# Local attention's scores and values in one burst of matmuls, the linear state in another

## The chip, the core and the metric

The kernel runs on one core of a Trainium2 chip. The metric is the device time of one execution in microseconds (us); runs of one kernel are compared by their median. The engines are named as in the profile: PE (TensorE, matmuls) with PEld (its weight loads), ACT (ScalarE), DVE (VectorE), POOL (GpSimd) and SP (SyncE, which here issues most DMAs). Matmul results land in PSUM, eight banks of 128 partitions x 512 fp32 values.

## What is computed

One input x of 2048 positions x 1024 goes through two attention blocks of 32 heads of 32, and a gate mixes their outputs. Block A is linear attention, block B looks at eight positions, two apart, behind each query.

```python
g = sigmoid((x * gate_w).sum(-1, keepdims=True))
# A: phi(t) = where(t > 0, t + 1, exp(t)) + 1e-6
q, k, v = split(x @ A_wqkv); pq, pk = phi(q), phi(k)
kv = einsum("bhsd,bhse->bhde", pk, v); z = pk summed over s
a = (einsum("bhqd,bhde->bhqe", pq, kv) / (einsum("bhqd,bhd->bhq", pq, z) + 1e-6)) @ A_wo
# B: for query s the keys s, s-2, ..., s-14 (those >= 0)
q, k, v = split(x @ B_wqkv)
b = (softmax(q . k[idx] * 32**-0.5) over the 8 keys, times v[idx]) @ B_wo
out = g * a + (1 - g) * b
```

## The kernel before

A small planner (`Prog`) takes every operation in program order with an estimated cost, its reads and writes and a priority (by default the place in program order). It simulates the five engines and writes out a fixed order for each; waits between engines are semaphores that follow from reads and writes. It does so six times, each time giving out PSUM banks by when the pass before freed them, and keeps the shortest plan. PE, like the others, runs its list strictly in order.

The stages, in PE's order:

1. Values of B for all positions (L1413 to L1428), 16 tiles x 2 halves of 8 matmuls of 128x512 ("a group"), stored to HBM with a column of ones behind each head's 32 values (33 columns a head).
2. Keys and queries of B, transposed (L1540 to L1556), first for the even, then for the odd positions (`e_` = 0, 1; dilation 2 makes the two halves independent, and x is read so that each half lies together). 32 groups each. For `e_` = 0 the gate's products run on DVE beside them; for both, DVE keeps running maxima and minima of q and k (`top`).
3. Local attention of B, cut into 9 blocks of up to 2 x 57 queries for each half, 18 in all (`FILLS`). It is spread over the large groups: after each group `slot` is called, which adds `FILL` = 0.2 to a pace, so that every fifth group is followed by the `fill` of one block; `after(n, f)` calls f n slots later.
4. Keys of A through phi (L1590 to L1600, 32 groups, the key loop): ACT takes the exponential of the bank, DVE a minimum, and DVE adds both from the bank (`phi`, L1364).
5. The linear state. `mT` = x^T phi(k) (L1653 to L1666): 8 column chunks x 2 halves of 16 matmuls, against chunks `xn` of x loaded in natural layout. Then the state of each head, `W_v`^T `mT` (`state`, L1635), and its product with A_wo (`fold`, L1680).
6. Queries of A, their scaling by the denominators, and the outputs of both blocks (`query`, `scaled`, `output`).

One block of local attention (`fill`, L1469) goes so. `spread` (L1461) copies the block's queries into `qx` twice, once on ACT and once on DVE, each masked to every other head. 32 matmuls of 64x64 tiles (`s_fn`, L1480) write the scores of 64 keys x 114 queries into the four banks `SO` = 4 to 7. ACT takes the exponential of the four banks into `E` (L1489), DVE multiplies the band mask on (L1492), and then `spread` is put into the program for the next block. Three slots later `values` (L1498) follows: 64 matmuls of 33 columns into the same four banks, the last column of a head being the softmax denominator; DVE takes the reciprocal of the denominators (L1514), multiplies (L1515), and two DMAs store the block to HBM, from where `turn` (L1454) reads finished tiles back transposed into `qT`, the left operand of the outputs. Large groups meanwhile take banks from `main` = banks 0 to 3 (L1445).

The state is made in eight pieces: three slots after each chunk of `mT`, `state(c)` adds the chunk's 32 matmuls of 128x32 tiles to one bank that DVE set to zero before; that bank is kept back from `main` (banks 0 to 2) while the `mT` loop runs. After the first two query groups of A the bank is copied to `kvT` (L1754), which `fold` reads.

At the start of the key loop (L1565 to L1587) DVE reduces the maxima and minima (`top_end`), which go to HBM and back as one row to make a flag: the kernel branches on it late, into a general path that the data don't take. The two first `xn` chunks (four DMAs) are loaded there too; their memory overlaps that of the maxima and of the gate's tiles.

Of the kernel before, what the change touches and what calls it, by code (L numbers as in the profile page):

```python
# [6 lines left out]
ACT = mybir.ActivationFunctionType  # L7
# [8 lines left out]
DH = 32  # L16
# [1103 lines left out]
def build_kernel(nc, A_x, A_wqkv, A_wo, B_x, B_wqkv, B_wo, gate_w, out):  # L1120
# [110 lines left out]
    rs = SB([128, 4, 8], F32, "rs")  # L1231
    ao = Ring([SB([128, 4, 8, 32], BF16, "ao%d" % i) for i in range(2)])
# [31 lines left out]
    def plan(seen):  # L1264
# [5 lines left out]

        class Pool:


            def __init__(self, bs):
                self.bs, self.n = bs, 0

            def next(self):
                if seen is None:
                    b = self.bs[self.n % len(self.bs)]
                else:  # L1280
                    b = min((b for b in self.bs if b.take is None or b.take in P.read), key=lambda b: seen[b.take] if b.take is not None else -1.0)
                self.n += 1
                b.take = len(takes)
                takes.append(len(P.ops))
                return b
# [36 lines left out]
        def top_end(i, op):  # L1322
            P.op("dve", lambda e: e.tensor_reduce(mx4[:, i:i + 1], mx[i][:, :], AX.X, op), 0.15 + mx[i].row / 960.0, reads=[mx[i].all()], writes=[mx4.part((i, i + 1))])
# [121 lines left out]
        main = Pool(banks[0:4])  # L1445
# [15 lines left out]
        def spread(e_, qs, nq, offs):  # L1461
            ready.append((e_, qs))
            rd = [pick.all(), qT.part((0, 8), (e_ * HS + qs, e_ * HS + qs + 2 * nq))]
            to = lambda i: qx[:, i, :, 0:2 * nq]
            of = lambda: qT[:, :, e_ * HS + qs:e_ * HS + qs + 2 * nq]
            P.op("act", lambda e: e.activation(to(0), of(), ACT.Copy, scale=pick[:, 0:1]), act(16 * nq), reads=rd, writes=[qx.part((0, 1), (0, 8), (0, 114))])
            P.op("dve", lambda e: e.tensor_scalar(to(1), of(), pick[:, 1:2], None, op0=ALU.mult), 0.1 + 16 * nq / 1920.0, reads=rd, writes=[qx.part((1, 2), (0, 8), (0, 114))])

        def fill(e_, qs, nq, offs):  # L1469
# [10 lines left out]
            def s_fn(e):  # L1480
                for c in range(8):
# [5 lines left out]
            P.op("pe", s_fn, 0.6, mode="r", reads=[kT.part((0, 8), (t0 + k0[0], t0 + k0[1] + 64)), qx.all()], writes=[s.iv for s in SO], name="S")  # L1487
            E, _ = Er.next()
            P.op("act", lambda e: e.activation(E[:, 0:32 * nq].rearrange("p (j q) -> p j q", j=4), ps[:, 4:8, 0:8 * nq], ACT.Exp), act(32 * nq),  # L1489
                 reads=[s.iv for s in SO], writes=[E.all()])  # L1490
            ev = lambda: E[:, 0:32 * nq].rearrange("p (g q) -> p g q", g=16)
# [3 lines left out]
            if todo:  # L1495
                spread(*todo[0])

            def values():  # L1498

                def each(e):  # L1500
                    for i in range(16):
                        for h in range(2):
                            for g in range(2):
                                hd = 16 * g + i
                                c, j = hd // 4, hd % 4
                                at = (j // 2 * 16 + 2 * c + j % 2) * nq
                                last = e.matmul(SO[2 * h + i // 8].ap(i % 8 * 33, i % 8 * 33 + 33)[64 * g:64 * g + nq, :], E[64 * h:64 * h + 64, at:at + nq],  # L1507
                                                vt[64 * h:64 * h + 64, hd * 33:hd * 33 + 33], start=True, stop=True, tile_position=(64 * h, 64 * g))
                    return last
                bi = [s.iv for s in SO]  # L1510
                P.op("pe", each, 0.6, mode="c", reads=[vt.all(), E.all()], writes=bi, name="PV")
                o_, k = ao.next()
                pv = lambda lo, hi: ps[:, 4:8, 0:264].rearrange("p b (i d) -> p b i d", d=33)[:, :, :, lo:hi]
# [345 lines left out]
```

## Time and profile before

| | us |
|---|---|
| median of 3 runs | 483.25 (482.88 to 484.38) |
| profiled execution | 483.49 |
| its span | 481.8 |

Busy time by stage of the profiled execution, as the profile counts it:

| stretch (us) | what runs | PE | DVE | ACT | POOL |
|---|---|---|---|---|---|
| 125.4 to 181.1 | odd keys and queries, local attention | 55.70 | 44.57 | 22.37 | 0.00 |
| 181.1 to 243.5 | key loop, local attention | 62.40 | 50.58 | 33.31 | 0.00 |
| 243.5 to 309.2 | `mT`, state, local attention | 65.70 | 28.40 | 22.48 | 32.94 |
| 339.1 to 442.7 | outputs and queries of A | 103.60 | 79.97 | 14.71 | 0.00 |

How to read the lines that follow: a group of instructions is named by line, engine and operation, then written tile <- read tiles, shapes and a count ("x32"), then total busy time in us and the mean of one in ns, then the engine's idle time before them and what ended it. The chain of waits is the work that ended last, followed back from the end; its pieces show start, length, engine and line. Matmuls are pipelined: the length shown for one is from its start to its modelled end, and matmuls in a row overlap, so distances between starts say what one costs. All matmuls of `group` have line L1360, whatever stage calls it.

### The profile page before, as it was taken

How to read it: one execution, taken by the hardware profiler on the slowest of the kernel's cores; microseconds unless marked ns; L12 is line 12 of the kernel's file. 1: busy time of each engine (PE TensorE's matmuls, PEld its weight loads, DVE VectorE, ACT ScalarE, POOL GpSimd, SP SyncE). 2: the span in 40 equal slices, each digit the busy share in tenths (PEclk: the TensorE clock that was granted, in tenths of full speed). 3: DMA queues.
4: the chain of work that ended last, by engine and by line, in shares of the span. 5: the costliest groups of instructions: out<-in, count | busy, mean ns of one | idle time of the engine just before them, and what ended most of it. 6: DMA issues, size and time to landing. Idle time of an engine off the chain costs nothing.

```text
span 481.8 us, 9606 instructions
## 1 busy us (share of the span) xinstructions
PE 476.6 (99%) x4162; PEld 224.9 (47%) x4162; DVE 308.9 (64%) x513; ACT 129.8 (27%) x176; POOL 39.4 (8%) x40
## 2 busy tenths in 40 slices
PE   9999999999999999999999999999999999999996
PEld 6444444444444444444444444444444444444444
DVE  2212176799877789877773325399987777677512
ACT  2111111112333435556533343244221000110000
POOL 3000000000000000000068551100000000000000
PEclk9999999999999999999999999999999999999999
DMA  9999998233123354373138554661423111241111
GB/s 237 214 215 289 327 321 245 73 102 98 35 57 74 103 136 110 87 184 74 46 87 197 138 141 88 172 191 33 89 66 66 44 45 44 71 63 44 46 44 48
DMA packets 95116, 57.09 MB, mean 118 GB/s; under 512 B 55385, under 2 KB 88538, under 8 KB 95066
## 3 DMA queue, kind: packets, MB, share of 16 engines
q1 hardware_dynamic: 94234, 55.61, 44.3%
q10 hardware_dynamic: 832, 0.79, 0.6%
q8 instruction: 34, 0.56, 0.5%
q14 instruction: 16, 0.13, 0.1%
HBM read 30.56 MB, written 12.72 MB: 90 GB/s over the span
## 4 chain that ended last, share of the span: by engine, by line
PE 99%; DVE 0%; issue 0%
PE ps_all L1360 58%; PE ps_all L1733 23%; PE ps_all L1661 12%; PE ps_all L1507 2%; PE ps_all L1484 2%; PE ps_all L1396 1%; PE ps_all L1640 1%; PE ps_all L1688 0%; DVE o L1390 0%
## 5 line engine op out<-in xcount | busy, mean ns | idle before, releaser
L1360 PE MATMUL ps_all<-w,xT 128*128 128x512 bf16 x512 | 113.1, 379 | 0.0
L1360 PE MATMUL ps_all<-xT,w 128*128 128x512 bf16 x512 | 112.6, 379 | 0.0
L1360 PEld LDWEIGHTS ps_all<-xT,w 128*128 128x128 bf16 x512 | 49.1, 98 | 58.5
L1360 PEld LDWEIGHTS ps_all<-w,xT 128*128 128x128 bf16 x512 | 48.9, 98 | 57.8
L1366 ACT ACTIVATE e<-ps_all 128x512 bf16<-128x512 f32 x64 | 38.2, 597 | 118.5 <-PE ps_all L1360 115.5
L1733 PE MATMUL ps_all<-kT,aT 128*128 128x512 bf16 (+1 forms) x264 | 60.7, 373 | 0.0
L1733 PE MATMUL ps_all<-w,qT 128*128 128x512 bf16 (+1 forms) x264 | 60.7, 373 | 0.0
L1360 PE MATMUL ps_all<-kT,xT 128*128 128x512 bf16 x256 | 57.9, 379 | 0.0
L1661 PE MATMUL ps_all<-pk,xn 128*128 128x512 bf16 x256 | 57.8, 380 | 0.0
L1387 DVE CAST vst<-ps_all 128x512 bf16<-128x512 f32 x16 | 11.1, 694 | 44.6 <-PE ps_all L1360 44.6
L1733 PEld LDWEIGHTS ps_all<-w,qT 128*128 128x128 bf16 x264 | 25.8, 98 | 29.7
L1733 PEld LDWEIGHTS ps_all<-kT,aT 128*128 128x128 bf16 x264 | 25.7, 98 | 29.5 <-issue 0.2
L1360 PEld LDWEIGHTS ps_all<-kT,xT 128*128 128x128 bf16 x256 | 24.7, 98 | 30.0 <-issue 0.7
L1390 DVE TENSOR_SCALAR o<-ps_all,gm 128x512 bf16<-128x512 f32 (+1 forms) x27 | 19.7, 731 | 28.2 <-PE ps_all L1733 28.2
L1661 PEld LDWEIGHTS ps_all<-pk,xn 128*128 128x128 bf16 x256 | 23.9, 98 | 27.6
L1489 ACT ACTIVATE E<-ps_all 128x1824 bf16<-128x1824 f32 (+1 forms) x18 | 30.4, 1688 | 16.7 <-PE ps_all L1484 16.7
L1367 DVE TENSOR_SCALAR e<-e 128x512 bf16<-128x512 bf16 x64 | 18.7, 294 | 23.2 <-ACT e L1366 23.1
L1623 POOL TENSOR_TENSOR zacc<-zacc,pk 128x1024 f32<-128x1024 f32 x15 | 31.9, 2127 | 16.3 <-DVE E L1492 15.5
L1388 ACT ACTIVATE kT<-ps_all 128x512 bf16<-128x512 f32 x24 | 13.8, 597 | 42.4 <-PE ps_all L1360 39.2
L1492 DVE TENSOR_TENSOR E<-E,msk 128x1824 bf16<-128x1824 bf16 (+1 forms) x18 | 20.5, 1140 | 4.1 <-ACT E L1489 4.1
L1388 ACT ACTIVATE vst<-ps_all 128x512 bf16<-128x512 f32 x16 | 9.6, 600 | 48.8 <-PE ps_all L1360 48.8
L1369 DVE SCALAR_TENSOR_TENSOR pk<-ps_all,e 128x512 bf16<-128x512 f32 x32 | 21.8, 685 | 0.7
(65 smaller groups left out, 343.3 us busy)
## 6 DMA issues: line engine op xcount, KB each, us to landing
v<-vB_hbm SPq DMA_DIRECT2D x36, 132.0 KB, 5.0
vB_hbm<-vst SPq DMA_DIRECT2D x32, 132.0 KB, 5.0
w<-in_B_wqkv_dram SPq DMA_DIRECT2D x4, 1024.0 KB, 9.4
xt<-in_A_x_dram SPq DMA_DIRECT2D x16, 256.0 KB, 5.4
w<-in_A_wqkv_dram SPq DMA_DIRECT2D x4, 1024.0 KB, 10.1
xn<-in_A_x_dram SPq DMA_DIRECT2D x8, 512.0 KB, 5.4
out_dram<-o SPq DMA_DIRECT2D x15, 256.0 KB, 2.0
oB_hbm<-ao SPq DMA_DIRECT2D x32, 114.0 KB
```

Source lines behind the costliest of these rows:

```text
L1360: last = e.matmul(bank.ap(), lhs(dc), rhs(dc), start=(dc == 0), stop=(dc == 7))
L1366: P.op("act", lambda e: e.activation(e_[:, :], bank.ap(), ACT.Exp), act(512), reads=[bank.iv], writes=[e_.all()])
L1367: P.op("dve", lambda e: e.tensor_scalar(e_[:, :], e_[:, :], 1.0, 1e-6, op0=ALU.min, op1=ALU.add), 0.25, reads=[e_.all()], writes=[e_.all()])
L1369: P.op("dve", lambda e: e.scalar_tensor_tensor(out=dst, in0=bank.ap(), scalar=0.0, in1=e_[:, :], op0=ALU.max, op1=ALU.add), dps(512), read ...
L1387: fd = lambda e: e.tensor_copy(dst, src())
L1388: fa = lambda e: e.activation(dst, src(), ACT.Copy)
L1390: fd = lambda e: e.tensor_scalar(dst, src(), scale, None, op0=ALU.mult)
L1489: P.op("act", lambda e: e.activation(E[:, 0:32 * nq].rearrange("p (j q) -> p j q", j=4), ps[:, 4:8, 0:8 * nq], ACT.Exp), act(32 * nq), rea ...
L1492: mk = P.op("dve", lambda e: e.tensor_tensor(ev(), ev(), m[:, :, :].rearrange("p r q -> p (r q)")[:, None, :].to_broadcast([128, 16, 2 * n ...
L1623: P.op("pool", lambda e, t=t: e.tensor_tensor(zacc[:, :], zacc[:, :], pkS[:, t, :], ALU.add), 2.2, reads=[src, zacc.all()], writes=[zacc.a ...
L1661: last = e.matmul(bank.ap(), tl[:, t, cs:cs + 128], pkS[:, t, r * 512:(r + 1) * 512], start=(t == 0), stop=(t == NT - 1))
L1733: last = e.matmul(bank.ap(0, f1 - f0), lh[:, k, t * 128:(t + 1) * 128], w[:, k, f0:f1], start=(first and k == 0), stop=(not first and k == 7))
```

## The change

- The values of a block no longer have a burst of their own. `fill` puts them into `pending`, and the next block's `burst` issues its 32 score matmuls and then the 64 value matmuls of the block in front as one PE operation. The first block's scores and the last block's values (three slots after its scores) stay alone.
- The values get banks of their own: 14 of 16 heads of each group go to `VO` = banks 2 and 3, the last two to columns 456 to 488 of the four `SO` banks, behind the scores. So a burst needs six banks. `Pool` gets `soon`: while a burst is two slots away or less, large groups may take banks 0 and 1 alone.
- The results are four DVE instructions (reciprocal and product for the 14, then for the 2); `rs` and `ao` are laid out anew for it. They come in the program behind the exponential of the scores of the same burst and ahead of its mask.
- `spread` for the next block comes three slots after the scores, and both its copies wait for the last PE operation planned by then.
- `top_end` halves its 1024 columns twice by `tensor_tensor` and reduces 256; the two calls, the flag's chain and the first `xn` loads come 6, 11, 12 and 12 slots into the key loop.
- The state's 256 matmuls are one PE operation after the first two query groups of A, and its order is changed: for each four heads all eight chunks in a row, the first of them starting the sum. The zeroed bank is gone, `main` has four banks in the `mT` loop (under the rule of `soon`), and the copy to `kvT` follows the burst.

```diff
-    rs = SB([128, 4, 8], F32, "rs")
-    ao = Ring([SB([128, 4, 8, 32], BF16, "ao%d" % i) for i in range(2)])
+    rs = SB([128, 2, 16], F32, "rs")
+    ao = Ring([SB([128, 2, 16, 32], BF16, "ao%d" % i) for i in range(2)])
...
             def next(self):
+                bs = self.bs[0:2] if self.soon is not None and self.soon() <= 2 else self.bs
...
         def top_end(i, op):
-            P.op("dve", lambda e: e.tensor_reduce(mx4[:, i:i + 1], mx[i][:, :], AX.X, op), 0.15 + mx[i].row / 960.0, reads=[mx[i].all()], writes=[mx4.part((i, i + 1))])
+            behind = [[o for o in P.ops if o.eng == "pe"][-1]]
+            for n in (512, 256):
+                P.op("dve", lambda e, n=n: e.tensor_tensor(mx[i][:, 0:n], mx[i][:, 0:n], mx[i][:, n:2 * n], op), 0.08 + n / 1920.0, reads=[mx[i].all()], writes=[mx[i].all()],
+                     after=behind)
+            P.op("dve", lambda e: e.tensor_reduce(mx4[:, i:i + 1], mx[i][:, 0:256], AX.X, op), dps(256), reads=[mx[i].all()], writes=[mx4.part((i, i + 1))])
...
         SO = banks[4:8]
-        main = Pool(banks[0:4])
+        VO = banks[2:4]
+
+        def soon():
+            if todo:
+                return max(1, int(-(-(1.0 - pace[0] - 1e-6) // FILL)))
+            return later[0][0] - slot_n[0] if pending and later else 99
+
+        main = Pool(banks[0:4], soon)
+        pending = []
+        pace = [0.0]
+        P.op("dve", lambda e: e.memset(SO[3].ap(456, 489), 1.0), 0.1, writes=[SO[3].iv])
...
+        def burst(s_fn, reads, cost):
+            v_fn, v_reads, results = pending.pop() if pending else (None, [], None)
+            for b in (VO if v_fn else []) + SO:
+                take(b)
+
+            def fn(e):
+                last = s_fn(e) if s_fn else None
+                return v_fn(e) if v_fn else last
+            P.op("pe", fn, cost + (0.48 if v_fn else 0.0), mode="r", reads=reads + v_reads, writes=[b.iv for b in (VO if v_fn else []) + SO], name="S" if s_fn else "PV")
+            if results:
+                afterwards.append(results)
...
-            P.op("pe", s_fn, 0.6, mode="r", reads=[kT.part((0, 8), (t0 + k0[0], t0 + k0[1] + 64)), qx.all()], writes=[s.iv for s in SO], name="S")
+            burst(s_fn, [kT.part((0, 8), (t0 + k0[0], t0 + k0[1] + 64)), qx.all()], 0.4)
...
+            while afterwards:
+                afterwards.pop()()
...
             if todo:
-                spread(*todo[0])
...
+                after(3, lambda f=todo[0]: spread(*f, behind=[[o for o in P.ops if o.eng == "pe"][-1]]))
+
+            def v_fn(e):
+                for i in range(16):
+                    for h in range(2):
+                        for g in range(2):
+                            hd = 16 * g + i
+                            c, j = hd // 4, hd % 4
+                            at = (j // 2 * 16 + 2 * c + j % 2) * nq
+                            to = VO[h].ap(i * 33, i * 33 + 33) if i < 14 else SO[2 * h + i - 14].ap(456, 489)
+                            last = e.matmul(to[64 * g:64 * g + nq, :], E[64 * h:64 * h + 64, at:at + nq],
+                                            vt[64 * h:64 * h + 64, hd * 33:hd * 33 + 33], start=True, stop=True, tile_position=(64 * h, 64 * g))
+                return last
...
+                for i0, i1, src, bs in ((0, 14, pv, vb), (14, 16, px, xb)):
+                    reg = [rs.part((h, h + 1), (i0, i1)) for h in range(2)]
+                    P.op("dve", lambda e, i0=i0, i1=i1, src=src: e.reciprocal(rs[:, :, i0:i1], src(32, 33).rearrange("p a b o -> p a (b o)")), 0.2, reads=bs, writes=reg)
+                    P.op("dve", lambda e, i0=i0, i1=i1, src=src: e.tensor_tensor(o_[:, :, i0:i1, :], src(0, 32), rs[:, :, i0:i1, None].to_broadcast([128, 2, i1 - i0, 32]), ALU.mult),
+                         dps(64 * (i1 - i0)), reads=bs + reg, writes=[o_.part((h, h + 1), (i0, i1), (0, 32)) for h in range(2)])
...
-            after(PVLAG, values)
...
+            def finish():
+                burst(None, [], 0.0)
+                afterwards.pop()()
+
+            pending.append((v_fn, [vt.all(), E.all()], results))
+            if not todo:
+                after(PVLAG, finish)
...
-        top_end(0, ALU.max)
-        top_end(1, ALU.min)
...
+        after(6, lambda: top_end(0, ALU.max))
+        after(11, lambda: top_end(1, ALU.min))
...
+            for o in P.ops[first:]:
+                o.prio += 40 if o.eng == "dve" else 0
+
+        after(12, fast_ok)
...
-        xns = [load_xn(0), load_xn(1)]
+        xns = []
+        after(12, lambda: xns.extend(load_xn(i) for i in range(2)))
...
-        main = Pool(banks[0:3])
-        sb = banks[3]
-        sb.take = len(takes)
-        takes.append(len(P.ops))
-        P.op("dve", lambda e: e.memset(sb.ap(0, 256), 0.0), dps(256), writes=[sb.iv])
-
-        def state(c):
+        def state():
+            sb = main.next()
+
             def fn(e):
                 for i in range(8):
-                    for j in range(4):
-                        h = 4 * i + j
-                        last = e.matmul(sb.ap()[32 * j:32 * j + 32, i * 32:i * 32 + 32], ws[0][:, c, h * 32:(h + 1) * 32], mT[:, c, h * 32:(h + 1) * 32],
-                                        start=False, stop=(c == 7), tile_position=(0, 32 * j), skip_group_check=True)
+                    for c in range(8):
+                        for j in range(4):
+                            h = 4 * i + j
+                            last = e.matmul(sb.ap()[32 * j:32 * j + 32, i * 32:i * 32 + 32], ws[0][:, c, h * 32:(h + 1) * 32], mT[:, c, h * 32:(h + 1) * 32],
+                                            start=(c == 0), stop=(c == 7), tile_position=(0, 32 * j))
                 return last
-            P.op("pe", fn, 0.22, mode="c", reads=[ws[0].part((c, c + 1), (0, 1024)), mT.part((c, c + 1), (0, 1024))], writes=[sb.iv], name="kv")
+            P.op("pe", fn, 2.1, mode="c", reads=[ws[0].all(), mT.all()], writes=[sb.iv], name="kv")
+            move(kvT[:, :, :].rearrange("p i d -> p (i d)"), lambda: sb.ap(0, 256), 256, sb, kvT.all())
...
-            after(3, lambda c=c: state(c))
...
-        move(kvT[:, :, :].rearrange("p i d -> p (i d)"), lambda: sb.ap(0, 256), 256, sb, kvT.all())
+        state()
```

72 lines of the change are left out of this document (33 added, 39 removed).

## The prediction

> **What bounds the kernel now.** I read the page's busy shares, clock and chain first, then the pieces of the chain in order of time, then single bursts.
>
> ```profile
> PE 476.6 (99%) x4162; PEld 224.9 (47%) x4162; DVE 308.9 (64%) x513; ACT 129.8 (27%) x176; POOL 39.4 (8%) x40
> PEclk9999999999999999999999999999999999999999
> q8 instruction: 34, 0.56, 0.5%
> PE 99%; DVE 0%; issue 0%
> ```
>
> TensorE is 99% of the chain, at full clock in every slice. No other engine's time is on the path, so the change is worth what it does to TensorE's own sequence, plus any wait that it brings in. The sequence itself, from the chain of waits (start, us, line, matmuls):
>
> ```profile
> 125.44 0.53 PE ps_all L1484 x32
> 125.97 5.29 PE ps_all L1360 x24
> 131.25 0.61 PE ps_all L1507 x64
> 131.87 3.56 PE ps_all L1360 x16
> ...
> 161.22 0.74 PE ps_all L1507 x64
> ...
> 243.67 1.73 PE ps_all L1661 x8
> ...
> 257.75 0.30 PE ps_all L1640 x32
> 261.61 0.61 PE ps_all L1507 x64
> 262.22 0.31 PE ps_all L1640 x32
> ...
> 312.83 0.31 PE ps_all L1640 x32
> ...
> 339.30 6.91 PE ps_all L1733 x32
> 346.20 3.45 PE ps_all L1360 x16
> ```
>
> The rows join end to end: between the scores (L1484), the values (L1507), the state (L1640) and the large matmuls nothing waits. One thing is paid beside arithmetic. Sixteen large matmuls take 3.45 where nothing lies between them and 3.56 where a burst follows; 24 take 5.29 against 6.91 x 24/32 = 5.18. So entering a burst costs 0.11. What leaving one costs lies inside the burst's own piece:
>
> ```profile
> 125.37 0.60 PE L1484 MATMUL ps_all<-qx,kT 64*64 64x114 bf16 x32
> 131.19 0.68 PE L1507 MATMUL ps_all<-v,E 64*57 64x33 bf16 x64
> 257.68 0.38 PE L1640 MATMUL ps_all<-mT,w 128*32 128x32 bf16 x32
> L1484 PE MATMUL ps_all<-qx,kT x576: 207/209/237, 125.4 to 299.1; 64*64 64x114 bf16 x172, 64*64 64x112 bf16 x20
> L1507 PE MATMUL ps_all<-v,E x1152: 174/178/200, 131.2 to 305.3; 64*57 64x33 bf16 x172, 64*56 64x33 bf16 x20
> L1640 PE MATMUL ps_all<-mT,w x256: 176/176/190, 257.7 to 313.0; 128*32 128x32 bf16 x128
> 131.18:131.51 0.33, 0.33 (x43) 1.00 0.00 0
> ```
>
> The first three are from the timeline, the next three give the length of one matmul (min/median/max, ns), the last counts the L1507 matmuls active in a stretch. A burst's length less one matmul is the time from its first start to its last: scores 0.60 - 0.21 = 0.39, values 0.68 - 0.18 = 0.50, state 0.38 - 0.18 = 0.20. The piece of the scores is 0.53, so 0.14 lie between its last start and the next large matmul. The last round of four needs 114 columns, at 6.91/32 = 0.216 per 512 columns 0.05; leaving costs 0.09. For the values it is 0.61 - 0.50 = 0.11, less a round of 0.03: 0.08.
>
> **The joined burst.** 576/32 = 18 score bursts and 1152/64 = 18 value bursts stand now. A pair costs 0.53 + 0.61 + 2 x 0.11 = 1.36. Afterwards the first scores and the last values stay alone and 17 bursts hold 32 + 64 matmuls. Both kinds work in 64-by-64 tiles (the 57 and 56 columns of the values fit a 64-wide one). If no turn is paid between them, a joined burst is 0.11 + 0.39 + 0.05 + 0.50 + 0.03 + 0.08 = 1.16: 0.20 saved, 3.4 for the 17. No row shows scores followed directly by values. The other end is that the turn stays. A state burst behind values pays none of the 0.11 in its neighbours' pieces (0.61, then 0.31), yet 0.61 is what values cost before large matmuls too: one turn of 0.08 to 0.09 between two kinds of tile instead of two. By that end a pair saves 0.11, the 17 save 1.9. I take 3.4, since the rows show turns only where the tile's shape changes (64x64, 128x32, 128x128) and none inside the values, whose four positions alternate. [...]
>
> **The state.** Eight bursts of 0.30 to 0.31 (the first and the last stand above) are 2.44; five follow another burst directly, three stand alone (257.75 and 312.83 are two of them) and pay 0.11 each: 2.77 together. One burst pays entry and exit once, 0.19. Its 256 matmuls cost 0.20/31 = 0.0065 each if they go on as 32 do: 1.6, a gain of 1.0. Against that, of the values 43 fall into the first 0.33, and the other 21 start in the 0.18 up to 131.69: 0.0086 each. A long burst slows down once it has run some 43 deep, and by that price 256 take 2.20. Then there is the piece of 0.74 among those of 0.61, 0.13 more with no engine named: I read it as a hitch in the supply of instructions, since a matmul and its weight load are two instructions of 64 bytes if the instruction queue's 0.56 MB in 34 packets carry them all (8,324), and one packet of 16 KB is 128 matmuls. Two such hitches in 256: 0.26. Together 2.65, a gain of 0.1, which I take, as 256 lie far past 43. [...] That consecutive matmuls of the new order add to the same 32 columns is in no row of small tiles; it is a rival below. Its copy to SBUF stays two large groups (3.45) ahead of the first fold that reads it.
>
> **What is costed at nothing, and its cover.** TensorE's queue holds all the large matmuls behind a burst, so any late input of a burst is paid in full.
>
> ```profile
> 215.40:225.40 10.00, 10.00 (x141) 4.79 (x144) 7.65 (x14) 5.46 (x7) 0.00 (x0) 1.00 0.36 65
> 211.20 0.68 PE L1507 MATMUL ps_all<-v,E 64*56 64x33 bf16 x64
> 211.30 0.60 ACT L1366 ACTIVATE e<-ps_all 128x512 bf16<-128x512 f32 x1 [1.13 <-PE ps_all L1360]
> 212.37 1.21 DVE L1515 TENSOR_TENSOR ao<-ps_all,rs 128x1024 bf16<-128x1024 f32 x1
> 213.50 0.68 DVE L1369 SCALAR_TENSOR_TENSOR pk<-ps_all,e 128x512 bf16<-128x512 f32 x1
> L1489 ACT ACTIVATE E<-ps_all 128x1824 bf16<-128x1824 f32 x16 | 27.1, 1691 | 15.1 <-PE ps_all L1484 15.1
> L1492 DVE TENSOR_TENSOR E<-E,msk 128x1824 bf16<-128x1824 bf16 x16 | 18.3, 1146 | 3.6 <-ACT E L1489 3.6
> L1466 ACT ACTIVATE qx<-qT,pick 128x912 bf16<-128x912 bf16 x16 | 16.7, 1047 | 2.0 <-DVE qT L1390 2.0
> L1514 DVE RECIPROCAL rs<-ps_all 128x32 f32<-128x32 f32 x18 | 6.4, 356 | 17.2 <-PE ps_all L1507 17.2
> ```
>
> Banks: the last two of the five groups ahead of a burst may take only banks 0 and 1, and the burst needs 2 and 3 read. Now the key group that ends at 211.1 has its bank read at 213.50 + 0.68, 3.1 later, behind a value result of 1.21. Afterwards the last group before a burst has the burst and one group, 1.16 + 1.73 = 2.9, until its bank is wanted, and value results begin only 1.2 after its end, when its chain (0.60, 0.3, 0.68 and the steps between, 1.9) is nearly through. The group just behind the burst is worse: the exponential (1.69) holds ScalarE, then results and mask (1.15) hold VectorE; by these rows its bank is read some 3.2 to 3.4 after its end, and group four wants it at 2 x 1.73 = 3.45. Covered, with little to spare.
>
> Copies of the queries (1.05 on ScalarE) move from right behind the scores to after the third group, which leaves two groups, 3.45, for 1.05 plus one 0.60 ahead of it. The results become four VectorE instructions for two, 0.3 to 0.4 more per burst by the 0.36 of a reciprocal of 32 columns, against 10.00 - 7.65 = 2.35 idle in such a stretch. The two long reductions of the maxima are cut into halvings and a short reduction and go 6 and 11 groups later; they fill the same idle time. ScalarE's exponential and mask start 0.55 later in the burst but have five groups until the values read them, where they had three.
>
> SyncE: four xn loads, the write and the read-back of the three maxima move 12 groups (some 23 us) into the key loop, whose 32 groups end at 243.67 and begin some 62 earlier. The read-back waits for the write on SyncE's queue, with v loads and result stores behind it:
>
> ```profile
> 184.29 0.57 SPq L1569 DMA_DIRECT2D mx_hbm<-mx  x1
> 188.48 0.23 SPq L1570 DMA_DIRECT2D mxr<-mx_hbm  x1
> DMA to landing us min/median/max: 3.7/5.4/8.0
> ```
>
> That is a hold of 4.2 before, and the same after, against the 9.8 from one burst to the next. The xn loads (8.0 at most to land) would start near 205 and are read by L1661 at 243.67. If that cover were gone, each microsecond late would be one on the path.
>
> **The sum.** The profiled execution took 483.49, its span 481.8, the rest lies outside. 483.49 - 3.4 - 0.1 = 480.0. The median of the three runs, 483.25, is 0.24 below it, so I forecast 479.8. Less than 0.3%, 1.45, could not be told from no change.
>
> **The rivals.**
> *The turn between scores and values stays.* 1.9 in place of 3.4: 481.5, as a median 481.3. For it: every row where one burst meets another shows a turn. Against: in all of them the tile's shape changes.
> *The state burst outruns its instructions.* Two 16 KB blocks are used in 2.2, while a fetch packet takes 0.5% x 16 x 481.8/34 = 1.13. With both fully exposed the state costs 0.19 + 2.20 + 2.26 = 4.65, 1.9 over now: 482.0, as a median 481.8.
> *Banks.* If the bank read of 3.4 slips past 3.45 by 0.5 in the six bursts of the key loop, where each bank needs two engines, 3.0 come back: 483.0, as a median 482.8. For it: the margin of 0.1. Against: VectorE idles a quarter of that stretch, and the other 11 bursts have single copies to read a bank.
> *Slower: the state's sums wait for themselves.* In L1640's new order eight rounds in a row add to the same columns. If each round must see the last one written, it costs one matmul's length, 0.176, in place of 0.026 to 0.034: 64 x 0.176 + 0.19 = 11.5 against 2.77, and 483.49 - 3.4 + 8.7 = 488.8, as a median 488.6. It decides from a round of 0.093 up ((3.4 + 2.77 - 0.19)/64), where the gain is gone. Against: large matmuls add to the same bank at 0.216 apart with no wait; for it, 0.026 is a spacing at which the trace has no such sum.
> That scores and values don't come together is excluded: they are one operation of the plan.
>
> **How the numbers follow.** Forecast 0.56, turn 0.15, instructions 0.08, banks 0.09, sums 0.08, anything else 0.04. The forecast's own range is 478.9 (state at its fast price) to 480.6 (a pair saves 0.15). The range asked for reaches over the turn, the instructions and the banks to 482.8 and down to 478.7. Faster by over 0.3% (under 481.8): 0.55 + 0.12 + 0.05 + 0.03 + 0.02 = 0.77. Slower: 0.08 + 0.02 of the banks + 0.02 = 0.12. The rest, 0.11, is no change.
>
> **What would show it.** In the chain: 17 pieces of 96 matmuls at about 1.05 (1.16 less the entry), near 1.15 with the turn; the piece ahead still 5.29 or 3.56; one L1640 piece of 256 at about 2.5, near 4.5 with fetches, over 10 with waiting sums. A bank wait would show as ScalarE or VectorE in the chain, or as a TensorE piece of 8 to 24 large matmuls longer than its count x 0.216 + 0.11. I am wrong if the joined pieces don't save 0.2 each, or if such longer pieces add up to over 2.

## The result, and the profile after

| | before | after |
|---|---|---|
| median of the runs side by side (us) | 483.25 (9 runs) | 487.35 (486.02 to 491.11, 9 runs) |
| ratio, 95% interval | | 1.0099 [1.0072, 1.0126] |
| profiled execution, its span | 483.49, 481.8 | 488.77, 486.9 |

The kernel became 1.0% slower; the forecast was 479.8. The profiled execution of the changed kernel lies 1.4 above its median, so the sizes below are those of a longer execution than most; its runs spread over 5 us, those of before over 1.8.

From the page of the changed kernel, busy times and the chain that ended last:

```profile
PE 470.9 (97%) x4115; PEld 227.3 (47%) x4162; DVE 316.5 (65%) x555; ACT 129.9 (27%) x174; POOL 40.2 (8%) x40
PE 95%; DMA 2%; issue 2%; DVE 1%
```

TensorE was 99% of the chain and is 95% now, with a DMA and VectorE in it. So the loss is waits, not matmuls. Where the joined bursts run undisturbed, the chain (start, us, line, matmuls) reads:

```profile
145.24 0.53 PE ps_all L1518 x32
145.77 0.51 PE ps_all L1542 x63
146.28 0.16 issue
146.44 8.58 PE ps_all L1368 x39
155.02 0.53 PE ps_all L1518 x32
```

Of each burst's 64 value matmuls and of the 40 large ones one record is missing, which the chain shows as 0.16 of issue. A cycle of five groups is 155.02 - 145.24 = 9.78; before it was 0.53 + 5.29 + 0.61 + 3.56 = 9.99. That is 0.21 a pair, 3.6 for 17. That scores pass into values without a turn is read from the starts in the timeline below: 213.59 and 214.03 are 0.44 apart, the 0.39 + 0.05 of the prediction, and nothing is left for the 0.09 of a turn.

The first loss lies in the key loop. The chain there:

```profile
203.90 0.52 PE ps_all L1518 x32
204.42 0.51 PE ps_all L1542 x63
...
205.08 5.14 PE ps_all L1368 x23
...
210.35 6.80 DMA mx_hbm<-mx
...
217.17 4.71 DMA mxr<-mx_hbm
...
221.90 0.65 DVE mx L1619
...
224.03 5.30 PE ps_all L1368 x16
229.33 0.53 PE ps_all L1518 x32
```

And the timeline of the same stretch (start, length, instruction; in brackets the idle time before it and who ended it):

```profile
213.59 0.60 PE L1518 MATMUL ps_all<-qx,kT 64*64 64x114 bf16 x32
...
214.03 0.67 PE L1542 MATMUL ps_all<-v,E 64*56 64x33 bf16 x64
...
217.04 1.69 ACT L1523 ACTIVATE E<-ps_all 128x1824 bf16<-128x1824 f32 x1 [2.74 <-PE ps_all L1368]
...
217.97 3.63 PE L1368 MATMUL ps_all<-w,xT 128*128 128x512 bf16 x16 [1.44 <-DVE pk L1377]
...
221.90 0.65 DVE L1619 TENSOR_REDUCE mx<-mxr 1x3 f32<-1x384 f32 x1 [1.91 <-DMA mxr<-mx_hbm]
...
224.01 2.38 PE L1368 MATMUL ps_all<-w,xT 128*128 128x512 bf16 x7 [2.41 <-DVE mx L1624]
```

The flag's maxima go to HBM in 6.80 and come back in 4.71, 11.5 together where the trace of before has 4.2 for the write. VectorE reaches the reduction of the row (L1619) at 219.99 (221.90 - 1.91) and stands until the row is there. The reads of the banks are behind it in VectorE's fixed order, TensorE has no bank to write, and stands 2.41. Some 5 us ahead there is another stand of 1.44: the joined burst's last matmul starts near 214.5, yet ScalarE's exponential and VectorE's reciprocal, which wait for its signal, start together at 217.04. In the trace's signals TensorE's own comes 2.5 behind the last start; behind every other burst it is 0.24. Behind both comes a third cost (window, TensorE busy; the 0.50 is the granted clock):

```profile
224.85:228.26 3.41, 3.41 (x9) 1.22 (x8) 1.74 (x5) 0.60 (x1) 0.00 (x0) 0.50 0.80 184
```

For 3.41 TensorE has half its clock and does 1.7 of work. From 203.90 to 229.33 two cycles take 25.43 in place of 19.56: 5.9 lost, as 1.6 + 2.6 + 1.7 (the stands as distances of starts less one matmul, 0.2 over the idle times).

The second loss is the state (chain; then the instruction queue in the stretch 315.4 to 318.5, packets, MB, share of 16 engines):

```profile
310.06 3.45 PE ps_all L1368 x16
313.52 1.88 PE ps_all L1690 x200
315.40 3.07 issue
318.47 0.59 PE ps_all L1690 x56
319.06 0.16 issue
319.22 3.40 PE ps_all L1368 x15
```

```profile
q8 instruction: 1, 0.02, 2.2%
```

200 matmuls go in 1.88, then nothing for 3.07 with no engine and no data named, then the other 56. The 0.16 behind them is a missing record again (15 of 16 large matmuls stand there). The transfers show one packet of instructions in the stand, from 316.13 to 317.23, and none in the 1.88 before it. In those 1.88 other data fill the 16 transfer engines (stretch 313.5 to 315.4):

```profile
q1 hardware_dynamic: 1247, 0.31, 99.9%
```

The state takes 319.06 - 313.52 = 5.54 in place of 2.77.

| part | forecast | in the profiled execution |
|---|---|---|
| 17 joined bursts | -3.4 | -3.6 |
| state | -0.1 | +2.8 |
| key loop, flag | 0 | +5.9 |
| first stage (0.84 to the first large matmul) | 0 | +0.8 |
| all else, most of it between the last result and the end of the span | 0 | -0.8 |
| span | -3.5 | +5.1 |

The first stage is before anything that the change touches: its piece was 5.46 before, is 6.21 here, and is 4.92 (four pieces, bound) and 6.12 (`xn` loads later) in kernels below. TensorE starts at about half its later rate (before, 31 matmuls in the 3.91 from 0.84 to 4.75 and 24 in the next 1.65); the record of the granted clock at 1.00 begins at 4.75 before and at 6.40 here, and half of that difference is the 0.8. Since the piece varies as much in kernels with this stage unchanged, it is counted as chance, not as an effect of the change. The rest of the table is two losses, to be explained apart.

### The profile page after: what moved, and what is told of

Read it like the earlier page. It is cut to its first block, busy times and chain, and to the rows that moved or that the text cites. A ratio compares the mean times of both kernels' runs of the same rounds, so it can differ in the third digit from the quotient of the medians.

```text
span 486.9 us, 9582 instructions
## 1 busy us (share of the span) xinstructions
PE 470.9 (97%) x4115; PEld 227.3 (47%) x4162; DVE 316.5 (65%) x555; ACT 129.9 (27%) x174; POOL 40.2 (8%) x40
## 4 chain that ended last, share of the span: by engine, by line
PE 95%; DMA 2%; issue 2%; DVE 1%
PE ps_all L1368 55%; PE ps_all L1783 23%; PE ps_all L1712 11%; PE ps_all L1518 2%; PE ps_all L1542 2%; DMA mx_hbm<-mx 1%; PE ps_all L1404 1%; DMA mxr<-mx_hbm 1%; PE ps_all L1690 1%; PE ps_all L1738 0%; DVE mx L1619 0%; DVE pk L1377 0%; DVE o L1398 0%; DVE e L1375 0%; DVE ao L1554 0%
## 5 line engine op out<-in xcount | busy, mean ns | idle before, releaser
L1368 PE MATMUL ps_all<-xT,w 128*128 128x512 bf16 x500 | 110.2, 379 | 1.2 <-issue 0.8
L1712 PE MATMUL ps_all<-pk,xn 128*128 128x512 bf16 x249 | 55.0, 379 | 1.1 <-issue 1.1
L1554 DVE TENSOR_TENSOR ao<-ps_all,rs 128x896 bf16<-128x896 f32 (+1 forms) x36 | 24.5, 682 | 0.2
L1377 DVE SCALAR_TENSOR_TENSOR p<-ps_all,e 128x512 bf16<-128x512 f32 x32 | 22.0, 689 | 0.7
```

The source lines that it names most:

```text
L1368: last = e.matmul(bank.ap(), lhs(dc), rhs(dc), start=(dc == 0), stop=(dc == 7))
L1377: P.op("dve", lambda e: e.scalar_tensor_tensor(out=dst, in0=bank.ap(), scalar=0.0, in1=e_[:, :], op0=ALU.max, op1=ALU.add), dps(512), read ...
L1554: P.op("dve", lambda e, i0=i0, i1=i1, src=src: e.tensor_tensor(o_[:, :, i0:i1, :], src(0, 32), rs[:, :, i0:i1, None].to_broadcast([128, 2, ...
L1712: last = e.matmul(bank.ap(), tl[:, t, cs:cs + 128], pkS[:, t, r * 512:(r + 1) * 512], start=(t == 0), stop=(t == NT - 1))
```

## The experiments

Theories: (A) VectorE's order has the flag's row too early, because the plan counts each of the two transfers as 2.5 us (a `lat` of 0.5 and 2.0 that it adds to every transfer); a rival is that the transfers only stand in a bad place. (C) The state's burst outruns its supply of instructions; the rival (D) is that its sums to the same columns wait for each other. The delayed signal near 216 had no theory at first; (E) was that the `xn` loads beside it cause it. Ratios are to runs of the kernel before on the same chip.

**The flag early again.** `top_end`, the flag's chain and the first `xn` loads go back to the start of the key loop, the joined bursts stay.

```diff
-        after(6, lambda: top_end(0, ALU.max))
-        after(11, lambda: top_end(1, ALU.min))
+        top_end(0, ALU.max)
+        top_end(1, ALU.min)
-        after(12, fast_ok)
+        fast_ok()
-        xns = []
-        after(12, lambda: xns.extend(load_xn(i) for i in range(2)))
+        xns = [load_xn(0), load_xn(1)]
```

> The changed kernel with the reductions of the maxima, the flag's chain and the first two xn loads put at the start of the key loop again, all else as changed. Theory A (VectorE stands in its strict order before the flag's read-back, which comes late beside the xn loads, so banks are not read and TensorE waits, then runs at half clock): the wait near 215 to 224 us is gone, about 5.9 us less than the changed kernel, near 481.5. Rival B (the rule of two banks and VectorE's greater load make TensorE wait in the key loop wherever the flag stands): no more than 1 us is gained, and TensorE still waits some us between 181 and 243.

489.61, 1.0112 [1.0079, 1.0145], where some 481.5 were expected. The stall goes along with the transfers (chain, then a window with its clock):

```profile
188.56 5.43 DMA mx_hbm<-mx
...
194.01 4.65 DMA mxr<-mx_hbm
...
198.69 0.65 DVE mx L1619
```

```profile
199.68:203.09 3.41, 3.10 (x8) 1.18 (x9) 2.90 (x10) 0.00 (x0) 0.00 (x0) 0.50 0.50 117
```

Moving the flag into the key loop is thus not what hurts; what hurts is a trip of 10 us in an order made for 5. That kernel has no delayed signal: its bursts end near 184.7 and 194.7, the write flies from 188.56 to 194.0.

**The state in four pieces, unbound; and both edits.** The 256 matmuls are cut into four operations of 64, two bands each, in a bank held back, with a query group between them in the program.

```diff
-        def state():
-            sb = main.next()
+        def state(k):
+            sb = banks[7]
...
-                for i in range(8):
+                for i in range(2 * k, 2 * k + 2):
```

> The changed kernel with the state's 256 matmuls cut into four bursts of 64 (two of the eight i each, same order inside), a query group of A between them, and the folds one to two groups later. Theory C (a burst uses up two blocks of 256 instructions faster than the next one can be fetched, and stands 3.07 us): no or little standing, the state's four pieces cost 4 x (0.11 + 0.50 + 0.08) = 2.4 to 2.8 where it costs 5.65 now, so about 3 us less than the changed kernel, near 484.4. Rival D (successive sums to the same 32 columns wait for each other): the order inside is the same, so the pieces still sum to over 5 us and nothing is gained.

> Both edits together: flag, reductions and xn loads at the start of the key loop, state in four bursts of 64. If A and C both hold, the rest of the change is the 17 joined bursts: 17 x 0.20 = 3.4 under the kernel before, plus 0.2 for the state, so 479.6 (ratio 0.9925 to the kernel before). If B or D holds instead, over 482.

489.29, 1.0133 [1.0080, 1.0187], and 487.58, 1.0079 [1.0051, 1.0107]. Neither answers its question: in both the planner drew the four pieces together again, and the chain of the first has 126 + 74 + 56 matmuls with a stand of 2.41 ahead of the last 56, as in the one burst.

**VectorE's part of the flag later.** The transfers stay; the reduction and what follows go into a function of their own, first by program place alone, then bound.

```diff
+        def fast_late():
...
+        after(20, fast_late)
```

> The changed kernel with the flag's VectorE chain alone (the reduction of the row read back and five small instructions) put 8 groups later in the program, at slot 20; the store, the read-back and the xn loads stay at slot 12. Theory A: the row has landed long before VectorE comes to it, so 2.4 us of waiting and the 1.7 us of half clock behind it go, 4 or more less than the changed kernel, under 483.5. If instead the store and the xn loads disturb other engines by themselves (the first wait of 1.4 us near 216.5, where TensorE's signal of a finished burst came 2.3 us late), 1.4 us of waiting stay in the trace.

487.18, 1.0086 [1.0056, 1.0116]. The plan, which thinks the row is there, took the reduction early all the same: VectorE waited 1.49 for it at 221.29. The place in the program does not move it.

```diff
+        def fast_read():
+            behind = [[o for o in P.ops if o.eng == "pe"][-1]]
-            P.op("dve", lambda e: e.tensor_reduce(mx1[:, :], mxr..., writes=[mx1.all()])
+            P.op("dve", lambda e: e.tensor_reduce(mx1[:, :], mxr..., writes=[mx1.all()], after=behind)
...
+        after(28, fast_read)
```

> The changed kernel with the flag's VectorE chain at slot 28 of the key loop and made to wait for the TensorE group in front of it, so that the planner cannot take it up as soon as its own estimate says that the row has landed (in flag_late_read it did that, and the row came 11.3 us after the store was issued). Theory A, sharpened (the place of the read-back in VectorE's order rests on an estimate of some 5 us for two DMA trips that take 9 to 11.5): the wait of VectorE for mxr, TensorE's wait behind it and the half clock are gone: 4 us less than the changed kernel in this place. The first wait of 1.4 us near 216 stays if it comes from the transfers started together at slot 12. Rival B: another wait of the key loop takes its place and the time stays.

485.45, 1.0045 [1.0027, 1.0063]: by the ratios 0.54%, 2.6 us, better than the changed kernel, where 4 were expected. No piece of `mxr` is left in the chain; the first of the two stands and the state's remain (chain):

```profile
214.26 1.81 PE ps_all L1368 x8
216.07 0.02 issue
216.09 0.07 DVE rs L1553
...
308.20 1.84 PE ps_all L1695 x200
310.05 3.50 issue
313.55 0.63 PE ps_all L1695 x49
314.18 6.17 PE ps_all L1368 x16
```

Only VectorE's order changed, and the wait for the row went: that part of A is shown. The other cycles of the key loop have their 40 large matmuls in 8.74 without a stand, so no other wait took its place. The last row shows what came with a stand of 3.50 here: 16 large matmuls in 6.17 in place of 3.45, since the clock is at 0.50 for 6.83 from 312.62. So here the state costs 3.5 + 2.7 over its instructions.

**The state in four pieces, bound.** As before, each piece and each fold tied behind the last TensorE operation planned.

```diff
-            P.op("pe", fn, 2.1, mode="c", reads=[ws[0].all(), mT.all()], writes=[sb.iv], name="kv")
+            P.op("pe", fn, 0.52, mode="c", reads=[ws[0].all(), mT.all()], writes=[sb.iv], name="kv", after=[[o for o in P.ops if o.eng == "pe"][-1]])
```

> The changed kernel with the state in four bursts of 64 that are made to wait for the group in front of each (in state4 the planner drew the four together again, since it prefers matmuls of one tile shape in a row, so that run says nothing of D), and each fold bound in the same way. Theory C (supply of instructions): each piece is under one block of 256 instructions and a group of 1.7 us lies between: four pieces of 0.5 to 0.6 us, no standing of 2 to 3 us, 3 us less than the changed kernel. Rival D (sums to the same columns): the pieces sum to over 5 us.

486.03, 1.0067 [1.0045, 1.0089]: 0.32%, 1.5 us, better than the changed kernel, where 3 were expected. Its profiled execution, at 483.16 the fastest of six, has both of the flag's stands (1.11 and 1.43 of idle) and no half clock behind them. The timeline of the state:

```profile
309.74 0.66 PE L1692 MATMUL ps_all<-mT,w 128*32 128x32 bf16 x64
310.34 1.90 PE L1368 MATMUL ps_all<-kT,xT 128*128 128x512 bf16 x8
312.17 0.66 PE L1692 MATMUL ps_all<-mT,w 128*32 128x32 bf16 x64
...
317.02 0.66 PE L1692 MATMUL ps_all<-mT,w 128*32 128x32 bf16 x64
```

The same sums in the same order, 64 matmuls in some 0.6, without a stand: D falls.

**The old order in one burst.** The other way round: one burst of 256, chunks outermost as before the change, the bank zeroed ahead and all matmuls adding.

```diff
-                for i in range(8):
-                    for c in range(8):
+                for c in range(8):
+                    for i in range(8):
...
-                                            start=(c == 0), stop=(c == 7), tile_position=(0, 32 * j))
+                                            start=False, stop=(c == 7), tile_position=(0, 32 * j), skip_group_check=True)
```

> The changed kernel with one edit: the 256 small matmuls of the state stay one burst but go in the order of before (eight bands inside each chunk, so that consecutive rounds add to different columns); the bank is zeroed ahead and all matmuls add to it. If the supply of instructions stops the burst: it still stands 1.8 to 3.5 us after some 200 matmuls and takes 4.5 to 6 in all. If the sums to the same columns were the cause: it takes 2.5 to 2.9 without a stand. The rest stays as in the changed kernel, so the time is 486 to 491 by the first and 483 to 488 by the second; the trace decides, not the time.

One execution, 491.98. Chain:

```profile
313.08 1.87 PE ps_all L1691 x200
314.95 3.94 issue
318.89 0.63 PE ps_all L1691 x50
```

Again 200, a stand, and the rest, though consecutive rounds now add to different columns. With the kernel above this rules D out and agrees with C: the burst in one piece stands and the pieces do not, whatever the order of the sums. A packet of instructions again lies in the stand, from 316.41 to 317.54, and TensorE goes on 1.35 after it; in all seven kernels with one burst it is 1.2 to 1.5. So the size of the stand goes by when the packet starts: here 1.46 after TensorE stopped, for 3.94; in the kernel with the read later by place at 312.08, 0.43 ahead of it, for 1.81. The other data in front of the packet may hold it up; no kernel was run without them, so their part in the size is open.

**Both cures.** The bound read of the row and the bound pieces together.

> Both edits. If A and C hold: the changed kernel's joined bursts with little else, 483.25 - 3.4 - 0.2 + 1.4 (first wait near 216, if it stays) = 481.2; 479.7 if it goes.

481.77 (479.96 to 485.74, 10 runs), 0.9974 [0.9951, 0.9998]: ahead of both kernels, of the one before barely. By the ratios the two cures gain 1.25% together and 0.54% and 0.32% alone; the half clock behind the state in the bound read shows one way in which the stand that is left can cost more. The delayed signal is still there (1.32 of idle at 216.91). Four kernels went after it.

**The `xn` loads later**, seven groups on (`after(12, ...)` becomes `after(19, ...)`).

> As both_bound, with the first two xn loads (2 MB) at slot 19, away from the store of the maxima and from the 2 MB of weights loaded at slot 12 or so. Theory E (the store of 1.5 KB and TensorE's late signal near 216 come from the bulk transfers in flight with it): the store lands in about 4.2 us as in the kernel before, the wait of 1.4 us is gone, near 479.7. Rival: the store itself, 128 pieces of 12 bytes, holds up the signals wherever it stands: the wait stays, 481.2.

481.99, 0.9974 [0.9952, 0.9996], and the stand is there: E falls.

**The write, or the weight loads of 1,024 KB issued next to it.** First the write alone, six groups later and bound; then both loads, eight groups later and bound; then only the load behind the write.

```diff
-        after(12, fast_ok)
+        after(18, fast_ok)
...
-... chan="mxo", lat=0.5)
+... chan="mxo", lat=0.5, after=[[o for o in P.ops if o.eng == "pe"][-1]])
```

> As the kernel with both cures (the flag's row read late, the state in four pieces), but the write of the maxima starts six groups later, behind two more of SyncE's issues, near 222 in place of 209.4. Open is the TensorE wait of 1.3 to 2.1 us near 215, which in each kernel so far ended as that write landed. If the write itself holds the signal behind the burst back: no idle stretch over 0.45 us near 215, and one of 1 to 2 us at the next burst that the write's landing meets, near 225 to 230; the time within 1 us of 481.8. If the weight load of 1,024 KB issued beside the write does it: the wait stays at 215. If neither, but the meeting of the two: no such wait anywhere, and the time is 480.0 to 480.6.

```diff
-                    aq.append(load_w(4, 0, Aw, 0, 50))
-                    aq.append(load_w(4, 1, Aw, 512, 51))
+                    aq.append(0)
+                    after(8, lambda: aq.extend([load_w(4, 0, Aw, 0, 50, after=...), load_w(4, 1, Aw, 512, 51, after=...)]))
```

> As the kernel with both cures, but the two weight loads of 1,024 KB that stand on either side of the write of the maxima are issued eight groups after their old place. If the write itself holds the signal back: the TensorE wait of 1.3 to 2.1 us near 215 stays, ending as the write lands. If the load does: it goes to the burst behind the load's new place, near 225 to 230. If it takes both: no such wait, the write lands in 4 to 5 us in place of 6.5, and the time is 480.0 to 480.6 in place of 481.8.

```diff
-                    aq.append(load_w(4, 1, Aw, 512, 51))
+                    after(8, lambda: aq.append(load_w(4, 1, Aw, 512, 51, after=...)))
```

> As the kernel with both cures, but only the second of the two weight loads of 1,024 KB, the one issued right behind the write of the maxima, goes eight groups later; the write keeps its place ahead of the burst at 212.7. If the write in flight is enough to hold the signal behind that burst back: the TensorE wait of 1.3 to 2.1 us near 215 stays and ends as the write lands. If it takes the load behind it: no wait over 0.45 us there, although the write still starts near 209 to 210 and its flight covers the burst. The time is 481.8 by the first and 480.0 to 480.6 by the second.

480.96, 0.9948 [0.9930, 0.9967]; 481.89, 0.9978 [0.9944, 1.0013]; 480.49 (480.36 to 480.55, 4 runs), 0.9941 [0.9925, 0.9956]. The stand is gone in the first two and stays in the third. From the timeline of the third:

```profile
210.14 0.57 SPq L1617 DMA_DIRECT2D mx_hbm<-mx  x1
...
213.90 0.67 PE L1542 MATMUL ps_all<-v,E 64*56 64x33 bf16 x64
...
216.03 0.23 SPq L1618 DMA_DIRECT2D mxr<-mx_hbm  x1
216.09 1.69 ACT L1523 ACTIVATE E<-ps_all 128x1824 bf16<-128x1824 f32 x1 [1.92 <-PE ps_all L1542]
```

SyncE's read-back starts when the write has landed, at 216.03, and the burst's signal takes effect at 216.09. The load behind the write is not needed for it. The stand is shorter here, 0.62 of idle in place of 1.32; that the load lengthens it is not shown, since with it the signals of other kernels came 1.5 to 2.8 behind the last start, and here 1.7. In the second kernel the write moved too, to 213.5, without intent: SyncE's list is one order. In all ten kernels where a joined burst ends after SyncE has issued the write and before it has landed, the signal is late. In three it is prompt: in the first here the write starts at 214.3, behind the burst of 212.6, and lands 7.6 later, ahead of the next at 222.4; in the second, and in the last kernel below, the burst ends (213.7, 213.8) while SyncE still issues the write (213.45 to 214.02, 212.53 to 213.92). That it is the write itself is likely, not shown: in the kernel before, the scores' burst of 187.15 also ended inside the write's flight (184.29 to 188.48) and its readers started at 187.80, promptly.

In the profiled execution of the second, 486.89, another stand appears, 4.7 of idle at the first fold. Its runs reach to 488.9. Chain:

```profile
314.28 1.60 POOL zb L1671
...
321.68 0.34 DVE kvT L1395
...
322.07 0.66 PE ps_all L1746 x14
```

It is pattern A once more: the normaliser z goes to HBM and back (4.5 each way here, a `lat` of 0.3 and 1.5 in the plan), POOL copies it, and VectorE, in its order, does z's first product and its reduction ahead of the copy of the state that the fold waits for.

**True prices in the plan.** Two kernels that change only what the plan believes. The first has the changed kernel's flag, unbound, with a `lat` of 5.0 and 4.5 for the maxima and 4.5 and 4.0 for z, and the state in bound pieces; the second has the write later and the prices of z alone.

```diff
-... chan="mxo", lat=0.5)
+... chan="mxo", lat=5.0)
-... chan="mxi", lat=0.5)
+... chan="mxi", lat=4.5)
-... chan="zo", lat=0.3, name="own", prio=51)
+... chan="zo", lat=4.5, name="own", prio=51)
-                 chan="zi", lat=1.5, name="own", prio=51)
+                 chan="zi", lat=4.0, name="own", prio=51)
```

> The changed kernel with the state in four bound pieces, and no edit to the flag but its prices: the plan counts the write and the read-back of the maxima at 5.0 and 4.5 us in place of 0.5 each, and the write and the read-back of the normaliser z at 4.5 and 4.0 in place of 0.3 and 1.5. If the stall at 220 to 224 came of VectorE's order being made with trips that are too short: the plan itself puts the reduction of the read-back some 10 us later and no VectorE wait for it is left (chain without a piece of mxr), and the time is 481 to 482.5, as with the bound read. If the place of the transfers were the cause, it would still stand there, and the time is 486. The wait near 215 stays, as the write keeps its place.

> The kernel with the maxima's write six groups later, and the trips of z priced at 4.5 and 4.0 us. In the last runs TensorE stood 1.49 and 5.05 us before the first fold, because VectorE, in its fixed order, waited for z (POOL's copy of it began at 309.3 and 313.8) ahead of the copy of the state. With the price the plan puts the copy of the state ahead of z's first product. If that is where the runs part: no TensorE stand before the folds, median 479.5 to 480.6 and the slowest run under 482.5. If the runs part elsewhere: the median stays at 481 and the range at 479.8 to 482.9.

484.05 (481.57 to 486.36), 1.0018 [0.9999, 1.0036], and 482.14 (480.89 to 484.21), 0.9977 [0.9964, 0.9990]. In the first, the plan puts the reduction a burst later by itself and no wait for `mxr` is left in the chain, as A says; but the time forecast for it, 481 to 482.5, is missed by 1.5. Its profiled execution, at 482.33, is one of its faster ones and shows 0.72 of idle near 215, 0.21 near 230 and 1.29 in the state's third piece, without which it would be near 479.7 (0.2 more for each of the first two, as above). The stand in the third piece (chain):

```profile
312.84 0.53 PE ps_all L1692 x55
313.37 1.29 issue
314.66 0.23 PE ps_all L1692 x8
```

One record is missing, so 56 matmuls lie ahead of it. With the two pieces before and eight large matmuls behind each, that is 64 + 8 + 64 + 8 + 56 = 200 from the start of the state, the same count as in one burst: by that count the stand belongs to a place in the sequence of instructions, and here a short burst met it.

In the second the copy of the state comes ahead of z's product as meant, yet the plan now sets two folds side by side and TensorE has 1.30 of idle between them: no gain. The spread of single runs is explained in part only. The mean granted clock on record for each run goes with some of it (changed kernel: 1.000 at 486.02, 0.988 at 491.11), but a run of the first kernel here took 485.10 at 1.000; what it stood for was not seen.

## Why the prediction was wrong

**The joined bursts**: right. 0.20 a pair was the step, 0.21 is measured, and no turn is paid from scores to values: 0.44 lie from the first score to the first value, where before 0.53 lay between the first score and the large matmul behind.

**Banks, copies, results**: costed at nothing, rightly. In each undisturbed cycle of 9.78 no VectorE or ScalarE piece is in the chain.

**The flag**: this step failed: "That is a hold of 4.2 before, and the same after, against the 9.8 from one burst to the next". It priced SyncE, on which the read-back waits, and not VectorE, which reads the row and has the bank reads behind it. Before, the write took 4.2 and VectorE came to the same reduction 4.4 after the read-back's start at 188.48, and did not wait (timeline of before):

```profile
192.91 0.65 DVE L1571 TENSOR_REDUCE mx<-mxr 1x3 f32<-1x384 f32 x1
```

The read-back takes 4.1 to 5.4 where the chains show it, so that cover was narrow. After, the trip takes 11.5, VectorE comes too soon, and the wait costs TensorE 2.6, and with the delayed signal's 1.6 and the half clock's 1.7 makes 5.9. The runs show the VectorE part by its removal (no wait for `mxr` left, 1.0045 for 1.0099), and that the place is not its cause (flag early, 489.61).

**The state**: "Together 2.65, a gain of 0.1". The instructions alone are 1.88 + 0.59 = 2.47 against 0.19 + 2.20 = 2.39, so the slow price was right. This step failed too: the term of 0.26 for two hitches was mis-sized, one stand of 3.07 (1.8 to 3.9 in the other kernels with one burst). The rival "outruns its instructions" came nearest to the trace, at 4.65 for a measured 5.54, with a chance of 0.08; its 481.8 held no loss in the key loop. It counted what a packet takes to move, 1.13; the trace shows that the packet also starts 0.73 after TensorE has stopped and that TensorE goes on only 1.24 after it has landed. That TensorE waits for that packet is the reading that fits these runs; no run shows it directly.
- *The rival on the slower side*, sums that wait for themselves: wrong, by the four pieces and by the old order in one burst. The kernel did come out slower, by two waits of which one was not on the list.

**Together**: the forecast's gain of 3.5 in the span came, 8.7 were lost in the two places (5.9 + 2.8). With both cures and the load moved the median is 480.49, within 0.7 of the forecast, and its trace has 0.8 more of the delayed signal left in it.

## What to carry to other kernels

Where a planner writes a fixed order, ask of every transfer that is moved not only what its queue holds up but which engine reads its result, what stands behind that read in the engine's list, and whether the trip that the plan assumes is the one in the trace; binding the read behind later work removed the wait here. Joining bursts of small matmuls paid here where the tile's shape stays (0.21 a pair in 64x64 tiles), and the 96 of a joined burst went through without a stand; 256 in one burst stood after 200, for 1.8 to 3.9. 96 is no safe length: a piece of 64 stood 1.29 (true prices), and the last values alone, 64 too, 0.72 in the kernel with both loads later. And look at the granted clock behind a stand on TensorE: half the clock behind it cost 1.7 more in the changed kernel's key loop and 2.7 more in the bound read, and nothing behind the changed kernel's 3.07 in the state.

## What the runs showed that was not expected

- Half clock after a stand: 3.41 long after stands of 1.4 and 2.4 within 8 us (changed kernel) and of 3.4 (flag early), 6.83 after one of 3.50 (bound read), none after the changed kernel's own 3.07 in the state or after 1.1 and 1.4 within 6 us (bound pieces). In the changed kernel the dip is 3.413 long, and two dips begin, within 0.03, at whole multiples of that from where the record of the full clock begins: 224.85 - 6.40 = 64 x 3.413 there, 312.62 - 5.42 = 90 x 3.413 in the bound read, where the dip has twice the length. So a dip does not follow from the stand's length alone in these runs; why it comes when it does is not shown.
- The write of the maxima, 128 pieces of 12 bytes, took 4.2 to 8.7 to land, and the signal of a TensorE burst that ended in its flight came up to 2.5 late (2.78 behind the last start in place of 0.24, with the `xn` loads later). Why is open.
- In a burst of 256 the stand came after matmul 200 in every kernel that had it in one piece, whatever the order of the sums, and at the same count in the sequence in the kernel whose third piece stood.
